# Chunked attention and a two-layer MLP on one core: 15 instead of 10 blocks of the first layer in seven products whose sums stay in PSUM, and a new order of all steps

## The chip, the cores and the metric

The kernel runs on one core of a Trainium2 chip (trn2). The metric is the device time of one execution in microseconds (us); lower is better.

## The reference

Heads of 64 columns, chunks of 64 tokens; the attention's output is the input of a two-layer MLP with a leaky ReLU between.

```python
q, k, v: (8, 8, 576, 64) float32              # batch, heads, tokens, columns
scores = q_c @ k_c.T / 8, per chunk of 64     # 9 chunks per batch and head
attn = exp(scores - max); attn /= sum + 1e-9
x = (attn @ v_c), heads side by side          # (4608, 512)
h = x @ w_in                                  # (512, 2048)
out = maximum(0.01 * h, h) @ w_out            # (4608, 512) float32
```

## The kernel before

The 4608 tokens are 36 groups of 128 (two chunks). For a group `u` the steps are: load q and k (`load_qk`, "g", DMAs issued by POOL that also convert to fp16), turn them (on TensorE, "tq"/"tk", or by a transposing DMA on SP's queue, "tdq"/"tdk"), copy q into a zero-padded tile QZ ("q"/"cq"), scores ("s", tile Sp), maximum ("m"), subtraction ("b"), exponential ("x"), sum and reciprocal ("z"), scaling ("n", tile en), transposing the weights ("e"+"c", or by DMA "d"), product with v ("v", tile xp) and the copy into `xT` ("a").

The MLP goes over blocks of tokens: `BLOCKS = 2 * [128] + 17 * [256]`. The first layer is either plain (`mm1`, "M" and "A": out tile hT, then the leaky ReLU on ACT into gT, "G") or, for blocks 9 to 18, done as seven half-size products instead of eight (`wide`, "V", L416; j, half s of the hidden columns, product number n). Their operands are sums of quarters of the weights (`w_in_sum`, "WS") and of the tokens (`x_sums`, "xs"). There the products 1, 6, 7 and 4 accumulate in one PSUM bank (xbank). After 1, 6 and 7, ACT copies the bank to SBUF (`wide_x`, "lx", L447, tile xkeep); DVE adds products 2, 5 and 3 to those copies (`wide_m`, "la", L453); the leaky ReLU (`leaky`, "lp", L435) then reads the sums from SBUF. That is 20 passes over 128x512 values for a block.

The second layer of all 256-token blocks is in seven products in the same way (`product`, "R", L227; weight sums TW, "W"; token sums SG, "sum", L203; `combine`, "comb"); blocks 0 and 1 use plain products (`mm2`, "B", tile oP, L462).

`idle` ("i") issues products of a constant tile `warm` that nobody reads; its argument counts columns in units of 128, three to a product (L686).

Every engine and every queue works its instructions in program order; the program order is written out by hand in the string `ORDER`, read from left to right. `BANKS` says which of the PSUM banks a tile takes. POOL's DMAs share eight semaphores in turn, so that the ninth issue waits for the first one's landing. All POOL loads up to g8 are issued ahead of anything in `ORDER` (`LOADS`).

Of the kernel before, what the change touches and what calls it, by code (L numbers as in the profile page):

```python
# [16 lines left out]
def kernel(  # L17
# [9 lines left out]
    nc = tc.nc  # L27
# [14 lines left out]
    VL = (4, 5, 6, 7)  # L42
    UX = 9
    G = 2 * CH

    BLOCKS = 2 * [128] + 17 * [256]
    EARLY = (2, 3, 4)
    LAST = len(BLOCKS) - 1
    HF, HM = NFC // 2, d_model // 2
    W0 = 9  # L50
    AMID = range(W0, 17)
    ONE = EARLY + tuple(range(16, len(BLOCKS)))
    ZMM = range(W0 - 2, 16)

# [3 lines left out]


# [5 lines left out]
    xT = sbp.tile([128, NT, RING], FP16, name="xT")  # L65
    qk: dict[int, tuple[bass.AP, bass.AP]] = {}

    made: set[tuple] = set()

    def need(*what):  # L70
        assert what in made, what

    def load_qk(u):

        both = []
        for name, src in (("q_in", q), ("k_in", k)):
            if u in PAIRED:
                t = sbp.tile([CH, H, 2, D], FP16, name=name, tag=name + "2", bufs=len(PAIRED))
            else:
                t = sbp.tile([128, H, D], FP16, name=name, tag=name, bufs=NIN)  # L80
            r0, r1 = u * G, (u + 1) * G
            cut = min(-(-r0 // S) * S, r1) if r0 % S else r1
            for a, z in ((r0, cut), (cut, r1)):
                if a < z:
                    rows = src[a // S, :, a % S:a % S + z - a, :]
                    if u in PAIRED:
                        to = t[(a - r0) // 2:(z - r0) // 2].rearrange("p h r d -> p h (r d)")
                        rows = rows.rearrange("h (p r) d -> p h (r d)", r=2)
                    else:
                        to, rows = t[a - r0:z - r0], rows.rearrange("h p d -> p h d")  # L90
                    nc.gpsimd.dma_start(out=to, in_=rows)  # L91
            both.append(t)
        qk[u] = tuple(both)

    def load_v_heads(b, m, h0, h1):
        if b >= NVB:
            need("batch", b - NVB)
# [4 lines left out]

    def load_v(b):
# [3 lines left out]
    def load_w_in(f0, f1):  # L107
        for m in range(2):
            nc.gpsimd.dma_start(
                out=w_inT[m * CH:(m + 1) * CH, :, f0:f1],  # L110
                in_=moe_w_in[m * d_model // 2:(m + 1) * d_model // 2, f0:f1].rearrange("(t d) f -> d t f", d=D),
            )

    def load_w_in_quarter(a):
        load_w_in(512 * a, 512 * a + 512)

    def load_w_out_quarter(a):
        load_w_out(4 * a, 4 * a + 4)
# [45 lines left out]
    SG: dict[tuple[int, int], bass.AP] = {}
    bank: dict[tuple[int, str], bass.AP] = {}
    kept: dict[tuple[int, str], bass.AP] = {}
    opened: set[tuple[int, str]] = set()

    def weight_sum(n):
        b11, b12 = w_outT[:, :HF, :HM], w_outT[:, :HF, HM:]  # L170
        b21, b22 = w_outT[:, HF:, :HM], w_outT[:, HF:, HM:]
        x, y = {1: (b12, b11), 2: (b22, TW.get(1)), 3: (b22, b12), 4: (b21, TW.get(2))}[n]
        TW[n] = sbp.tile([128, HF, HM], FP16, name=f"TW{n}")
        nc.vector.tensor_tensor(out=TW[n], in0=x, in1=y, op=ALU.subtract)

    def rows(j):

        nh = BLOCKS[j] // 2
        halves_of = slice(0, nh), slice(nh, 2 * nh)
        return halves_of[::-1] if j in EARLY else halves_of  # L180

    def token_sums(j, n):
        if (j, n) in SG:
            return
        if j in EARLY:
            for a, p in {
                1: [(a, 1) for a in range(4)], 2: [(0, 2), (1, 2)], 3: [(0, 1), (1, 1), (0, 2), (1, 2)], 4: [(2, 2), (3, 2)],
            }[n]:
                need("act", j, a, p)
        if n in (2, 4):  # L190
            token_sums(j, n // 2)
        nh = BLOCKS[j] // 2
        one, two = rows(j)
        a11, a12 = gT[j][:, :HF, one], gT[j][:, HF:, one]
        a21, a22 = gT[j][:, :HF, two], gT[j][:, HF:, two]
        SG[j, n] = sbp.tile([128, HF, nh], FP16, name="SG", tag="gS", bufs=4, padded_shape=[128, HF, 128])
        x, y, op = {
            1: (a21, a22, ALU.add),
            2: (SG.get((j, 1)), a11, ALU.subtract),
            3: (a11, a21, ALU.subtract),  # L200
            4: (a12, SG.get((j, 2)), ALU.subtract),
        }[n]
        (nc.gpsimd if (j, n) in SG_POOL else nc.vector).tensor_tensor(out=SG[j, n], in0=x, in1=y, op=op)  # L203

    def product(j, n, i):
        one, two = rows(j)
        g, w = gT[j], w_outT
        where, left, right = {
            1: ("X", g[:, :HF, one], w[:, :HF, :HM]),
            2: ("W", g[:, HF:, one], w[:, HF:, :HM]),  # L210
            3: ("Z", SG.get((j, 4)), w[:, HF:, HM:]),
            4: ("X", g[:, HF:, two], TW.get(4)),
            5: ("Z", SG.get((j, 1)), TW.get(1)),
            6: ("X", SG.get((j, 2)), TW.get(2)),
            7: ("X", SG.get((j, 3)), TW.get(3)),
        }[n]
        if where != "X" and j in ONE:
            where = n
        if (j, where) not in bank:
            tag = None if j in EARLY else {"X": "qp", "Z": None if j in ZMM else "kp"}.get(where)  # L220
            bank[j, where] = psp.tile([128, 2, HM], FP32, name=f"pr{where}", tag=tag or mm(), bufs=1)
        to = bank[j, where]
        if j == LAST and n == 4:
            last_product(left, right)
            return
        for f in range(HF):
            nc.tensor.matmul(  # L227
                out=to[:, i, :],
                lhsT=left[:, f, i * 128:(i + 1) * 128],
                rhs=right[:, f, :],  # L230
                start=(j, where) not in opened,
                stop=(f == HF - 1),
                skip_group_check=True,
            )
            opened.add((j, where))

    def last_product(left, right):

        r0 = START[LAST] + BLOCKS[LAST] // 2
        for c in range(0, HM, HM // 2):  # L240
            cut = slice(c, c + HM // 2)
            of = psp.tile([128, HM // 2], FP32, name="prL", tag=mm(), bufs=1, padded_shape=[128, 512])
            for f in range(HF):
                nc.tensor.matmul(
                    out=of, lhsT=left[:, f, :128], rhs=right[:, f, cut], start=(f == 0), stop=(f == HF - 1)
                )
            to = ob[LAST, False][:, 0, cut]
            nc.vector.tensor_tensor(out=to, in0=of, in1=kept[LAST, 7][:, 0, cut], op=ALU.add)
            nc.sync.dma_start(out=out[r0:r0 + 128, cut], in_=to)

    def combine(j, n):
        made.add(("comb", j, n))
        if n == 3 and j in ONE:
            need("comb", j, 0)
        nt = BLOCKS[j] // 256
        half = lambda t: t[:, :nt, :]
        keep = lambda: sbp.tile([128, 1, HM], FP32, name="keep", tag="k_in2" if n == 6 else "q_in2", bufs=len(PAIRED))
        if n in (1, 6, 7):
            kept[j, n] = keep()
            nc.scalar.activation(out=half(kept[j, n]), in_=half(bank[j, "X"]), func=AFT.Copy, bias=0.0, scale=1.0)  # L260
            return
        if n == 0:

# [609 lines left out]
```

## Time and profile before

| what | value |
|---|---|
| time, median of 3 runs | 275.1 us (274.96 to 275.74) |
| span of the profiled execution, first to last instruction | 273.3 us |
| the median less that span (the page gives no other time of the profiled execution) | 1.8 us |
| TensorE busy | 265.9 us, 97%, 3705 products |
| DVE, ACT, POOL busy | 219.9 us (80%), 208.8 us (76%), 165.3 us (60%) |
| POOL's DMA queue | 18.10 MB |
| granted TensorE clock | full in each of the 40 slices |

A row of the page's groups reads: line, engine, operation, output<-input, shape, count, busy time in all, mean of one in ns, idle time of the engine ahead of them and who ended it. PE is TensorE's products, PEld its weight loads. A product's time in such rows includes its latency, so the pace of products is read from the chain of waits, where products follow each other.

### The profile page before, as it was taken

To read this page: it belongs to the slowest core of one execution; us is meant where nothing else is said; L and a number is where in the kernel's file an instruction comes from. 1 tells how busy PE (TensorE), PEld (TensorE's weight loads), DVE (VectorE), ACT (ScalarE), POOL (GpSimd) and SP (SyncE) were. 2 spreads that over 40 slices of the span, in tenths; PEclk is the share of its full clock that TensorE was granted. 3 is DMA by queue.
4 is the path that set the end of the run, shared out by engine and by line. 5 is a ranking of instruction groups with operands and counts; after the bars stand their busy time and mean duration, and the time that the engine had idled before them with its cause. 6 is when DMAs were issued, how large, how long until landed. Compare 5 with 4: busy or idle time off the path is not lost.

```text
span 273.3 us, 9009 instructions
## 1 busy us (share of the span) xinstructions
PE 265.9 (97%) x3705; PEld 242.4 (89%) x3705; DVE 219.9 (80%) x427; ACT 208.8 (76%) x410; POOL 165.3 (60%) x190
## 2 busy tenths in 40 slices
PE   7889999999999999999999999999999999999994
PEld 3579958999999899998989999999999998999994
DVE  7786869999997668798677987977899879488783
ACT  6667635665779688666999989899999998857560
POOL 8848546783175448649689799689895636012100
PEclk9999999999999999999999999999999999999999
DMA  9999999999999999999999999799999503131113
GB/s 147 155 188 191 206 178 156 176 117 130 210 138 169 171 140 119 195 219 168 164 189 153 203 160 124 139 134 180 95 147 158 134 2 101 22 98 40 41 41 115
DMA packets 159241, 38.34 MB, mean 140 GB/s; under 512 B 150240, under 2 KB 154720, under 8 KB 159200
## 3 DMA queue, kind: packets, MB, share of 16 engines
q0 software_dynamic: 111392, 18.10, 98.3%
q1 hardware_dynamic: 46768, 19.41, 38.7%
q8 instruction: 29, 0.48, 0.7%
q10 hardware_dynamic: 1040, 0.26, 0.4%
q14 instruction: 12, 0.10, 0.2%
HBM read 36.70 MB, written 9.44 MB: 169 GB/s over the span
## 4 chain that ended last, share of the span: by engine, by line
PE 86%; DVE 5%; ACT 3%; POOL 3%; issue 2%; POOLq 0%; DVEq 0%; ACTq 0%
PE hT L319 20%; PE prX L227 20%; PE xbank L416 11%; PE xpr L416 9%; PE prZ L227 6%; PE pr L227 6%; PE prW L227 3%; PE Sp L584 3%; PE xp L656 3%; PE oP L462 3%; ACT QZ L539 1%; ACT gT L435 1%; PE kp L512 1%; PE qp L512 1%; POOL SG L203 1%
## 5 line engine op out<-in xcount | busy, mean ns | idle before, releaser
L319 PE MATMUL hT<-xT,w_inT 128*128 128x128 f16 (+1 forms) x768 | 62.4, 237 | 0.0
L319 PEld LDWEIGHTS <-w_inT 128*128 128x128 f16 x768 | 53.6, 98 | 2.8
L227 PEld LDWEIGHTS <-SG 128*128 128x128 f16 x544 | 51.0, 98 | 5.4
L620 POOL TENSOR_TENSOR en<-ex,zi 128x512 f16<-128x512 f16 x26 | 28.2, 1085 | 40.1 <-DVE zi L614 19.8
L453 DVE TENSOR_TENSOR xkeep<-xpr,xkeep 128x512 f32<-128x512 f32 x60 | 39.6, 681 | 13.7 <-ACT xkeep L447 9.6
L333 ACT ACTIVATE gT<-hT 128x512 f16<-128x512 f32 x64 | 36.6, 595 | 9.0 <-PE hT L319 8.9
L227 PEld LDWEIGHTS <-gT 128*128 128x128 f16 x400 | 37.3, 98 | 4.3 <-ACT gT L435 0.4
L447 ACT ACTIVATE xkeep<-xbank 128x512 f32<-128x512 f32 x60 | 34.6, 593 | 7.4 <-PE xbank L416 7.0
L416 PEld LDWEIGHTS <-WS 128*128 128x128 f16 x640 | 38.0, 98 | 0.5
L91 POOL DMA_DIRECT2D q_in<-in_q_dram x39 | 33.4, 861 | 7.0 <-DMA w_outT<-in_moe_w_out_dram 3.0
L91 POOL DMA_DIRECT2D k_in<-in_k_dram x39 | 32.6, 838 | 7.8 <-DMA VB<-in_v_dram 3.3
L227 PE MATMUL prX<-TW,SG 128*128 128x256 f16 x272 | 35.3, 273 | 0.0
L435 ACT ACTIVATE gT<-xkeep 128x512 f16<-128x512 f32 x56 | 33.4, 631 | 2.1 <-DVE xkeep L453 1.8
L260 ACT ACTIVATE keep<-prX 128x256 f32<-128x256 f32 x51 | 19.6, 384 | 16.9 <-PE prX L227 16.5
L416 PEld LDWEIGHTS <-w_inT 128*128 128x128 f16 x480 | 29.0, 98 | 0.9 <-issue 0.4
L203 DVE TENSOR_TENSOR SG<-gT 128x1024 f16<-128x1024 f16 x34 | 25.2, 740 | 4.7 <-ACT gT L333 2.9
L610 DVE TENSOR_REDUCE z<-ex 128x8 f32<-128x512 f16 x36 | 24.4, 679 | 4.9 <-ACT ex L604 4.7
L593 DVE TENSOR_REDUCE mx<-Sp 128x8 f32<-128x512 f32 x36 | 24.4, 677 | 4.5 <-PE Sp L584 4.5
L573 ACT ACTIVATE QZ<-QT 64x512 f16<-64x512 f16 x44 | 27.3, 627 | 0.9 <-PE Sp L584 0.3
L677 ACT ACTIVATE xT<-xp 128x512 f16<-128x512 f32 x36 | 21.5, 596 | 6.0 <-PE xp L656 5.8
L387 POOL TENSOR_TENSOR xs<-xT 128x256 f16<-128x256 f16 x18 | 12.5, 701 | 20.7 <-ACT xT L677 20.7
L98 POOL DMA_DIRECT2D VB<-in_v_dram x24 | 23.4, 987 | 0.0
(92 smaller groups left out, 486.0 us busy)
## 6 DMA issues: line engine op xcount, KB each, us to landing
out_dram<-osb SPq DMA_DIRECT2D x35, 256.0 KB, 4.1
q_in<-in_q_dram POOLq DMA_DIRECT2D x31, 128.0 KB, 5.9
k_in<-in_k_dram POOLq DMA_DIRECT2D x31, 128.0 KB, 6.7
VB<-in_v_dram POOLq DMA_DIRECT2D x8, 288.0 KB, 9.1
VB<-in_v_dram POOLq DMA_DIRECT2D x16, 144.0 KB, 5.3
w_inT<-in_moe_w_in_dram POOLq DMA_DIRECT2D x8, 256.0 KB, 7.2
w_outT<-in_moe_w_out_dram POOLq DMA_DIRECT2D x4, 512.0 KB, 11.6
q_in<-in_q_dram POOLq DMA_DIRECT2D x8, 64.0 KB, 6.3
```

The source lines that it names most:

```text
L91: nc.gpsimd.dma_start(out=to, in_=rows)
L203: (nc.gpsimd if (j, n) in SG_POOL else nc.vector).tensor_tensor(out=SG[j, n], in0=x, in1=y, op=op)
L227: nc.tensor.matmul(out=to[:, i, :], lhsT=left[:, f, i * 128:(i + 1) * 128], rhs=right[:, f, :], start=(j, where) not in opened, stop=(f == ...
L319: nc.tensor.matmul(out=hT[:, i, :], lhsT=w_inT[:, t, fc * 128:(fc + 1) * 128], rhs=xT[:, t, r0:r0 + tb], start=(t == 0), stop=(t == NT - 1),)
L333: nc.scalar.activation(out=gT[j][:, nf * a:nf * a + nf, c0:c0 + tb], in_=HT.pop((j, a, p)), func=AFT.Prelu, bias=0.0, scale=1.0, alpha=0.01,)
L416: nc.tensor.matmul(out=to[:, i, :], lhsT=left[:, t, i * 128:(i + 1) * 128], rhs=right[:, t], start=(n in (1, 2, 5) and t == 0 and i == 0), ...
L435: nc.scalar.activation(out=gT[j][:, f0:f0 + 4, hi * 128:hi * 128 + 128], in_=of, func=AFT.Prelu, bias=0.0, scale=1.0, alpha=0.01)
L447: nc.scalar.activation(out=XK[j, s, n], in_=XB[j, s], func=AFT.Copy, bias=0.0, scale=1.0)
L453: nc.vector.tensor_tensor(out=to, in0=of, in1=to, op=ALU.add)
L573: nc.scalar.activation(out=to, in_=QT[u][part], func=AFT.Copy, bias=0.0, scale=1.0)
L593: nc.vector.tensor_reduce(out=MX[u], in_=SP[u], axis=AXL.X, op=ALU.max)
L620: (nc.gpsimd if u >= UP else nc.vector).tensor_tensor(out=E[u], in0=ex, in1=ZI.pop(u).unsqueeze(2).to_broadcast((128, 8, CH)), op=ALU.mult)
```

## The change

First layer: blocks 3 to 17 (15 blocks) in seven products; blocks 0 to 2 plain, in pieces of 128 tokens. All blocks have 256 tokens, so the second layer of all 18 is in seven products. In the first layer product 2 now accumulates onto a copy of product 1 in another PSUM bank ("ls", `wide_seed`); product 5 is copied to SBUF once ("lf", `wide_five`); DVE makes two sums per half ("la", `wide_add`), one of them back into the PSUM bank on which product 3 then accumulates. The leaky ReLU reads PSUM or the one copy. That is 16 passes for a block. A step marked with ' in `ORDER` goes to the other engine of its kind (ACT or DVE for copies, POOL or DVE for sums and "n"). Any of the eight PSUM banks may hold any tile (`ps`), and `sb` picks an SBUF slot by a digit of `BANKS`, too.

```diff
-    BLOCKS = 2 * [128] + 17 * [256]
-    EARLY = (2, 3, 4)
+    BLOCKS = 18 * [256]
+    LATE = (0, 1, 2)
+    def ps(shape, name, kind=FP32):
+        ...
+        return psp.tile(shape, kind, name=name, tag="m" + next(banks), bufs=1, padded_shape=padded)
+    def copy(other, to, of):
+        if other:
+            nc.vector.tensor_copy(out=to, in_=of)
+        else:
+            nc.scalar.activation(out=to, in_=of, func=AFT.Copy, bias=0.0, scale=1.0)
-    def wide_x(j, s, n):
-        ...
-        nc.scalar.activation(out=XK[j, s, n], in_=XB[j, s], func=AFT.Copy, bias=0.0, scale=1.0)
-    def wide_m(j, s, n):
-        ...
-        nc.vector.tensor_tensor(out=to, in0=of, in1=to, op=ALU.add)
+    def wide_seed(j, s, other=0):
+        XW[j, s] = ps([128, 4, 128], "seed")
+        copy(other, XW[j, s], XB[j, s])
+    def wide_five(j, s, other=0):
+        X5[j, s] = sb([128, 4, 128], FP32, "x5", "xkeep", 6)
+        copy(other, X5[j, s], XZ[j, s])
+    def wide_add(j, s, n):
+        to = XZ[j, s] if n == 3 else X5[j, s]
+        nc.vector.tensor_tensor(out=to, in0=XB[j, s], in1=X5[j, s], op=ALU.add)
+    def wide_leaky(j, s, n, other=0):
+        second, hi = {2: (0, 0), 4: (0, 1), 3: (1, 0), 5: (1, 1)}[n]
+        of = {2: XW, 4: XB, 3: XZ, 5: X5}[n][j, s]
+        ...
     ORDER = (
-        "i33 y4 y2 I y0 y6 y1 tq0 q0.0 q0.1 w3 tk0 i5 k0 i6 s0 tq1 i4 m0 b0 q1.1.1 i13 tk1 q1.0.1 x0 k1 tq2 i8 s1 tk2 "
+        "g2 y4 y5' y0' i110.0 g1 I If g3 tq0 y2' tk0 y3' k0 tq2 q0.0 tk2 tq1 q0.1' s0 i16.4 k2 y1 i14.3 q2.0 q2.1' s2 "
+        "q1.0 m0 b0 q1.1 tk1 x0 k1 tq3 q3.1 g6 i8.2 tq6 tk3 tk6 g5 m2 b2 q3.0 z0.0 s1 tq5 i17.7 m1 tk5 b1 k3 z0.1' i25.5 "
```

Three places of the order show the move. First TensorE at the start of the program: before, the end of the first run of idle products, after 11 of them (warm is the constant tile, q_f and k_f the first group of q and k).

```order
L686 LDWEIGHTS warm
L686 MATMUL idle<-warm 128x384
L512 MATMUL qp<-ident_139,q_f 128x128 x4
L512 MATMUL kp<-ident_139,k_f 128x128 x4
L686 LDWEIGHTS warm
```

Now the same place, after 36 idle products of 384 columns and one of 256:

```order
L194 MATMUL idle<-warm 128x256
L222 MATMUL qp<-ident_85,q_f 128x128 x4
L222 MATMUL kp<-ident_85,k_f 128x128 x4
L227 LDWEIGHTS q_in
L227 MATMUL qp<-ident,q_in 64x2x32
```

The first transposition has moved behind 26 more idle products. Second, POOL's queue behind the third group of loads; before, v and all of w_in go ahead of w_out with nothing between:

```order
L98 DMA VB_63<-in_v_dram 64x36x64 x2
L109 DMA w_inT<-in_moe_w_in_dram 64x4x512 x4
L91 DMA q_in<-in_q_dram 64x8x64 x2
L91 DMA k_in<-in_k_dram 64x8x64 x2
L109 DMA w_inT<-in_moe_w_in_dram 64x4x512 x4
```

Now (en is the scaling of group 1, a POOL instruction that waits for DVE):

```order
L122 DMA VB_63<-in_v_dram 64x36x64 x2
L117 DMA q_in<-in_q_dram 64x8x64 x2
L117 DMA k_in<-in_k_dram 64x8x64 x2
L140 DMA w_inT<-in_moe_w_in_dram 64x4x512 x2
L309 TENSOR_TENSOR en<-ex,z_405 128x512
L140 DMA w_inT<-in_moe_w_in_dram 64x4x512 x2
L117 DMA q_in<-in_q_dram 128x8x64
L117 DMA k_in<-in_k_dram 128x8x64
L140 DMA w_inT<-in_moe_w_in_dram 64x4x512 x2
```

Two quarters of w_in and the loads behind them have moved behind a step that waits. Third, DVE in the middle of the program, before, with the adds of products 2, 5 and 3:

```order
L281 TENSOR_TENSOR osb_3871<-prW,keep 128x256
L453 TENSOR_TENSOR xkeep<-xpr,xkeep 128x512
L610 TENSOR_REDUCE z<-ex 128x8
L612 TENSOR_TENSOR ze<-z,tiny 128x8
L614 RECIPROCAL zi<-ze 128x8
L203 TENSOR_TENSOR SG<-gT 128x1024
L598 TENSOR_TENSOR Sp<-Sp,mx 128x512
```

Now, where DVE also copies:

```order
L461 TENSOR_TENSOR x_3657<-xbank,x_3657 128x512
L198 COPY seed<-xbank 128x512
L461 TENSOR_TENSOR xz<-xbank,x_3796 128x512
L299 TENSOR_REDUCE z_3830<-ex 128x8
L198 COPY keep<-prX 128x256
L305 RECIPROCAL z_3838<-z_3835 128x8
L461 TENSOR_TENSOR xz<-xbank,x_3840 128x512
L418 TENSOR_TENSOR xs<-xT 128x256
```

Copies from PSUM and token sums have come to DVE; the small add ahead of the reciprocal has gone to ACT.

More of the change, by code (lines that the diff above doesn't have):

```diff
@@ L176, in rows @@
[L176 to L183, printed above, removed]
-            return
[L185 to L235, printed above, removed]
@@ L497, with idle @@
+    def idle(n, _=0):
+        t = ps([128, 512], "idle")
+        for i in range(0, n, 3):
+            c = 128 * min(3, n - i)
+            nc.tensor.matmul(out=t[:, :c], lhsT=warm[:, :128], rhs=warm[:, :c], start=True, stop=True)
+    def copy(other, to, of):
+        if other:
+            nc.vector.tensor_copy(out=to, in_=of)
+        else:
+            nc.scalar.activation(out=to, in_=of, func=AFT.Copy, bias=0.0, scale=1.0)
     QP: dict[int, bass.AP] = {}
@@ L735, with stage_a, hidden, part_of @@
-    ORDER = (
[84 rows of a table removed]
+    def stage_a(u, other=0):
+        at = u * G % RING
+        copy(other, xT[:, :, at:at + G], XP[u])
+        groups.add(u)
+    gT: dict[int, bass.AP] = {}
+    HT: dict[tuple[int, int, int], bass.AP] = {}
+    def hidden(j):
+        if j not in gT:
+            gT[j] = sb([128, NFC, BLOCKS[j]], FP16, "gT", "gT", 3, padded_shape=[128, NFC, NB])
+        return gT[j]
+    def part_of(j, p):
+        return (128, (p - 1) * 128) if p else (BLOCKS[j], 0)
+    def mm1(j, a, p=0):
+        tb, c0 = part_of(j, p)
+        rows_ready(START[j] + c0, START[j] + c0 + tb)
+        r0 = (START[j] + c0) % RING
+        nf = 512 // tb
+        hT = ps([128, nf, tb], "hT")
+        for i in range(nf):
+            fc = nf * a + i
+            for t in range(NT):
+                nc.tensor.matmul(
+                    out=hT[:, i, :],
+                    lhsT=w_inT[:, t, fc * 128:(fc + 1) * 128],
+                    rhs=xT[:, t, r0:r0 + tb],
+                    start=(i == 0 and t == 0),
+                    stop=(t == NT - 1),
+                    skip_group_check=True,
+                )
+        HT[j, a, p] = hT
@@ new lines, in halves_of, with token_sums @@
+    def halves_of(j):
+        both = slice(0, 128), slice(128, NB)
+        return both[::-1] if j in LATE else both
+    def token_sums(j, n, other=0):
+        one, two = halves_of(j)
+        g = hidden(j)
+        a11, a12 = g[:, :HF, one], g[:, HF:, one]
+        a21, a22 = g[:, :HF, two], g[:, HF:, two]
+        x, y, op = {
+            1: (a21, a22, ALU.add),
+            2: (SG.get((j, 1)), a11, ALU.subtract),
+            3: (a11, a21, ALU.subtract),
+            4: (a12, SG.get((j, 2)), ALU.subtract),
+        }[n]
+        SG[j, n] = sb([128, HF, 128], FP16, "SG", "gS", 5)
+        (nc.gpsimd if other else nc.vector).tensor_tensor(out=SG[j, n], in0=x, in1=y, op=op)
```

702 lines of the change are left out of this document (280 added, 422 removed), and 172 rows, old and new, of the table ORDER.

## The prediction

> **What bounds the kernel now.** I read the page's busy times first, then a table of five stretches, then the list of waits.
>
> ```profile
> PE 265.9 (97%) x3705; PEld 242.4 (89%) x3705; DVE 219.9 (80%) x427; ACT 208.8 (76%) x410; POOL 165.3 (60%) x190
> PEclk9999999999999999999999999999999999999999
> ```
>
> ```profile
> core 0: us, PE busy (x) PEld busy (x) DVE busy (x) ACT busy (x) POOL busy (x), PEclk, DMA share, GB/s
> 0.00:20.00 20.00, 16.41 (x237) 11.16 (x238) 15.66 (x33) 12.96 (x19) 14.26 (x25) 1.00 1.62 162
> 20.00:60.00 40.00, 40.00 (x603) 35.48 (x601) 32.80 (x62) 24.93 (x50) 28.17 (x34) 1.00 1.98 172
> 60.00:130.00 70.00, 70.00 (x852) 64.16 (x851) 57.51 (x115) 51.17 (x101) 40.15 (x44) 1.00 1.79 165
> 130.00:200.00 70.00, 69.82 (x1041) 66.15 (x1040) 57.12 (x111) 66.02 (x133) 59.14 (x65) 1.00 1.54 154
> 200.00:270.00 70.00, 69.66 (x985) 65.41 (x983) 56.74 (x107) 53.76 (x111) 23.56 (x25) 1.00 0.46 77
> ```
>
> From 20 to 270 us TensorE is idle for 0.52 us in all (0.18 + 0.34). So the end is set by two things only: how many products there are and at what pace they go, and what the first 20 us hold. The pace stands in the chain of waits, where products follow each other:
>
> ```profile
> 22.68 3.58 PE hT L319 x64
> 37.58 4.32 PE oP L462 x20
> 90.16 0.87 PE prX L227 x8
> 145.25 0.89 PE xbank L416 x16
> ```
>
> A product of 128 columns takes 55.9 ns (3.58/64, and 0.89/16 in the seven-product layer), one of 256 columns 109 ns (0.87/8), one of 512 columns 216 ns (4.32/20). Time goes by columns, with a little on top for each product.
>
> **The change: TensorE's work.** Counts are from code and order, prices from the rows above.
> - First layer. Before: 512 products of 128 columns (plain, in pieces), 256 of 256 (blocks 5 to 8), 1120 of 128 (ten blocks of 112). After: 384 plain of 128 and 15 x 112 = 1680. That is 432 more of 128 columns (+24.1 us) and 256 fewer of 256 columns (-27.9): -3.8 us.
> - Second layer. 1000 products of 256 columns instead of 944 (+6.1), none of the 32 of 512 columns (-6.9): -0.8 us.
> - Three groups less are turned on TensorE, 24 products of 128 columns: -1.3 us. Three groups more go by SP's transposing DMAs, and SP issues nothing else that early.
>
> The sum is -5.9 us. Scores, v products and the six groups whose weights TensorE turns stay.
>
> **The change: idle products.** The start reads:
>
> ```profile
> 1.33 3.50 PE L686 MATMUL idle<-warm 128*128 128x384 f16 x11 [1.33 <-DVE zeros L137]
> 4.71 0.63 PE L512 MATMUL qp<-ident,q_f 128*128 128x128 f32 x4
> 11.59 2.07 PE L686 MATMUL idle<-warm 128*128 128x384 f16 x13
> 17.44 1.95 PE L319 MATMUL hT<-xT,w_inT 128*128 128x128 f16 x32
> 20.05 1.06 PE L319 MATMUL hT<-xT,w_inT 128*128 128x128 f16 x16
> ```
>
> The first 11 idle products take 0.32 us each (3.50/11). The later 13, which hold 29 units of 128 columns, take 2.07, with the last one's latency: at most 71 ns a unit. I take 54 ns a unit (a quarter of the 216 above). The orders hold 111 units before and 239 after. Before: 3.5 + 78 x 0.054 = 7.7 us. After: the first run is 110 units, so 33 units go in 3.5 us and 77 in 4.2, to 9.0 us; the other 129 units take 7.0. In all 14.7 us, +7.0 us. This is the largest loss: the first transposition, which began at 4.71 us when its data had come, begins at 9.0.
>
> The Trainium skill (TensorE: Matmul & The Clock Gate, What's actually happening) says that the clock opens after about 3.4 us of work, in a window that runs free of the kernel. The trace agrees: slow to 4.8 us, fast behind. Should the window fall later, some ten more of the long first run would go at 0.32 instead of 0.16: +1.6 us. I do not count it; before, that would have hidden behind the wait for q.
>
> **The change: waits at the start.** Before, from 1.33 to 20.05 us: 18.7 us, of which 7.7 idle products and 6.1 of use (32 first-layer products 1.8, the rest turns, scores, v): 4.9 us are waits. The chain behind them:
>
> ```profile
> 7.87 0.69 DVE L593 TENSOR_REDUCE mx<-Sp 128x8 f32<-128x512 f32 x1 [0.50 <-PE Sp L584]
> 8.25 1.49 ACT L539 ACTIVATE QZ<-qp 64x512 f16<-64x512 f16 x2 [1.50 <-PE qp L517]
> 8.60 0.69 DVE L598 TENSOR_TENSOR sh<-Sp,mx 128x512 f32<-128x512 f32 x1
> 9.61 0.60 ACT L604 ACTIVATE ex<-sh 128x512 f16<-128x512 f32 x1
> 10.24 0.69 DVE L610 TENSOR_REDUCE z<-ex 128x8 f32<-128x512 f16 x1 [0.95 <-ACT ex L604]
> 13.28 0.67 DVE L620 TENSOR_TENSOR en<-ex,zi 128x512 f16<-128x512 f16 x1
> ```
>
> With these prices I put the new order's steps behind each other by hand, each when its engine and its input are free: scores of group 0 at 11.3 us (behind k's copy and q's cast on ACT, 0.6 each, from 10.0), of group 2 at 13.2, of group 1 at 15.4; scaling of group 0 done at 18.2, of group 1 (on POOL) at 20.4, of group 2 at 22.9; v products at 20.9, 23.6 and 24.4; copy of group 1's result, behind an exponential on ACT, done at 25.1. The first first-layer product goes at 25.2, where work and idle products alone come to 22.5, and one more wait of 0.35 follows. So 3.1 us of waits: -1.8 us. Much of what was waiting is idle products now.
>
> **What hides the rest.** ACT loses 60 copies of 593 ns and gains 47 like them; DVE keeps 60 adds.
>
> ```profile
> L453 DVE TENSOR_TENSOR xkeep<-xpr,xkeep 128x512 f32<-128x512 f32 x60 | 39.6, 681 | 13.7 <-ACT xkeep L447 9.6 <-PE xpr L416 3.9
> L447 ACT ACTIVATE xkeep<-xbank 128x512 f32<-128x512 f32 x60 | 34.6, 593 | 7.4 <-PE xbank L416 7.0 <-DMA out_dram<-osb 0.2
> L203 POOL TENSOR_TENSOR SG<-gT,SG 128x1024 f16<-128x1024 f16 x8 | 17.4, 2173 | 9.3 <-DVE SG L203 4.0 <-ACT keep L260 2.7 <-ACT xkeep L447 2.6
> L260 ACT ACTIVATE keep<-prX 128x256 f32<-128x256 f32 x51 | 19.6, 384 | 16.9 <-PE prX L227 16.5
> L387 DVE TENSOR_TENSOR xs<-xT 128x256 f16<-128x256 f16 x2 | 0.6, 282 | 0.0
> L387 POOL TENSOR_TENSOR xs<-xT 128x256 f16<-128x256 f16 x18 | 12.5, 701 | 20.7 <-ACT xT L677 20.7
> L541 DVE COPY QZ<-qp 64x512 f16<-64x512 f16 x19 | 7.9, 417 | 1.8 <-ACT QZ L539 1.5 <-PE qp L512 0.2
> L612 DVE TENSOR_TENSOR ze<-z,tiny 128x8 f32<-128x8 f32 x36 | 6.6, 182 | 1.2
> L281 DVE TENSOR_TENSOR osb<-prZ,keep 128x256 f32<-128x256 f32 x22 | 9.3, 421 | 4.6 <-PE prZ L227 3.1 <-ACT keep L260 1.2
> L620 POOL TENSOR_TENSOR en<-ex,zi 128x512 f16<-128x512 f16 x26 | 28.2, 1085 | 40.1 <-DVE zi L614 19.8 <-ACT xkeep L447 9.8 <-ACT gT L435 3.0
> ```
>
> DVE gains 19 copies of 256 values (0.42 each, 8), 19 of 512 (0.68, 13), 29 short token sums (0.28, 8); it gives away 8 long sums (0.7), 25 small adds (0.18), 15 q copies (0.42) and 4 clearings, some 19 in all. With some 2 us of small ones: about 232 us, 86% of 270. ACT comes to some 203, POOL to 184 (12 long sums more at 2.17). None passes TensorE; the same DVE held 82% from 20 to 60 and from 60 to 130 us while TensorE stood still for nothing. A copy from PSUM to PSUM is not in the trace: 0.38 us (half the columns, to SBUF) and 0.68 (the DVE add) bound it; I take the 0.593 of the same read. At 26 on ACT the ends are -5.5 and +2.3 us of ACT time, under 203 of 272: no cost to TensorE.
>
> In the order, between a product and the next that needs its bank read out, at least 1.3 us of other products stand now, 0.87 before. So I take 0.3 us of late waits instead of 0.52: -0.2. The last product, the two adds behind it and the two small stores stay as they were.
>
> **Sum.** -5.9 + 7.0 - 1.8 - 0.2 = -0.9: a span of 272.4 against 273.3. With the 1.8 us by which the median stands over that span: 274.2 us.
>
> **Rivals.**
>
> 1. The shared port makes it slower. One row pair shows what it costs:
>
> ```profile
> 204.40 1.98 DVE L203 TENSOR_TENSOR SG<-gT 128x1024 f16<-128x1024 f16 x1
> 204.76 1.06 POOL L620 TENSOR_TENSOR en<-ex,zi 128x512 f16<-128x512 f16 x1
> ```
>
> A DVE sum of two SBUF tiles, begun just ahead of a POOL instruction, ends only behind it: 1.98 us instead of about 0.7. POOL's sums and scalings grow to 20 long ones (2.17), 25 scalings (1.09) and 27 short (0.7): 89 us of 270, a third of the time, beside some 110 such DVE steps. Were they placed without regard to each other, about 36 would be hit. A hit lasts up to 2.2 us and the least distance on TensorE is 1.3, so up to 0.9 reaches TensorE each; if a sixth of them do that, +5.4 us: 279.6. Two that reach TensorE already end the gain. Against it: the order before has 70 such POOL steps, and TensorE idles for half a microsecond.
>
> The Trainium skill (SBUF — State Buffer, Who interferes with whom) states it as a rule: the port pair is an exclusive lock, and a DVE step with both inputs in SBUF blocks against a GpSimd step that reads SBUF. The trace agrees with the pair above. By that rule, more long sums on POOL speak against this change.
>
> 2. The start costs less: my hand chain has waits that cover each other, since q's first copies no longer stand behind the clearing of tiles on DVE. With 1.1 us of waits at the start instead of 3.1: 272.2.
>
> 3. The transfers are not further ahead where it counts: the second quarter of w_in now stands on POOL's queue behind the scaling of group 1.
>
> ```profile
> 15.02 0.68 POOL L91 DMA_DIRECT2D k_in<-in_k_dram  x1 [2.17 <-DMA VB<-in_v_dram]
> w_inT<-in_moe_w_in_dram POOLq DMA_DIRECT2D x8, 256.0 KB, 7.2
> ```
>
> In my chain POOL comes to that scaling at 15.3 us and may run it only at 19.4, so that quarter is issued until 21.7 and lands, with the 7.2 us of the row, at 28.9, where TensorE wants it at 28.8; each us on it is lost. Two us late: 276.2. For it: POOL waits for DMAs at the start as it is (2.17 us in one place). Against it: the queue has drained by then, so the landing should be quicker.
>
> **How the numbers follow.** The sum holds within a microsecond or so: 0.5. Shorter start: 0.18. Port: 0.2. Late weights: 0.12. Changes under 0.3% (0.8 us) can hardly be told from none, so the likeliest case lies on the edge: of its 0.5, 0.28 is faster, 0.18 the same, 0.04 slower. Faster: 0.28 + 0.17 = 0.45. Same: 0.18 + 0.01 + 0.04 = 0.23. Slower: 0.2 + 0.08 + 0.04 = 0.32. The likeliest case by itself spans 273.0 to 275.6. The range goes from 271.0 (all waits gone: -5.9 + 7.0 - 4.9 - 0.3 = -4.1) to 280.0 (the port's 279.6).
>
> **What would show it.** Right: TensorE's first transposition near 9 us and its first first-layer product near 25; from there on TensorE idle for under a microsecond; plain products near 56 ns. Wrong: idle of TensorE behind DVE sums or seeds in the middle (port, or the 128-column products at more than 56 ns), first-layer products waiting for w_in before 35 us, or a first transposition well before 9 us.

## The result and the profile after

The changed kernel takes 301.2 us (298.8 to 304.2), the kernel before 275.1 us beside it: a ratio of 1.091 (1.086 to 1.095), 9% slower where 274.2 us was forecast. The profiled execution is the longest of the four: 304.2 us, span 302.3. Here and below, a time is the median of all executions of a kernel and a ratio leaves out those more than 1.5% above its fastest, so the two can differ a little.

The first part of the page, busy times and granted clock:

```profile
PE 273.7 (91%) x3924; PEld 250.2 (83%) x3924; DVE 228.3 (76%) x456; ACT 203.0 (67%) x408; POOL 182.3 (60%) x192
PEclk9999999999999999999989999999997999999999
```

The table by stretches, cut as before (the last row is longer now):

```profile
core 0: us, PE busy (x) PEld busy (x) DVE busy (x) ACT busy (x) POOL busy (x), PEclk, DMA share, GB/s
0.00:20.00 20.00, 16.76 (x200) 10.77 (x201) 8.64 (x18) 12.36 (x20) 14.71 (x24) 1.00 1.91 156
20.00:60.00 40.00, 36.43 (x632) 33.63 (x628) 34.58 (x68) 32.13 (x66) 25.40 (x30) 1.00 1.49 150
60.00:130.00 70.00, 61.13 (x883) 56.54 (x884) 56.87 (x120) 50.94 (x103) 49.53 (x55) 1.00 2.03 147
130.00:200.00 70.00, 62.64 (x908) 58.37 (x907) 55.21 (x112) 51.94 (x106) 49.77 (x50) 0.98 1.76 165
200.00:270.00 70.00, 67.86 (x972) 64.33 (x970) 54.79 (x106) 44.37 (x92) 35.53 (x31) 0.98 0.55 86
```

DVE, ACT and POOL are as busy as forecast. TensorE is not: from 20 to 270 us it stands still for 3.57 + 8.87 + 7.36 + 2.14 = 21.9 us, where before it was 0.5. That is most of the 29.0 us by which the span grew. Three quarters of it (16.2 us) lie between 60 and 200 us, while loads are under way (POOL's last one lands at 228 us). The chain of waits, by engine:

```profile
PE 50%; DMA 27%; DVE 10%; ACT 9%; issue 3%; SPq 1%; DVEq 0%; ACTq 0%
```

TensorE had 86% of it before, and DMA none. Five of the chain's long pieces (start, length, what):

```profile
83.91 7.86 DMA et<-en
...
97.14 10.09 DMA KT<-k_in
...
109.63 10.27 DMA et<-en
...
130.62 9.36 DMA QT<-q_in
...
141.36 8.17 DMA et<-en
```

All three names are transposing DMAs that SP issues: et turns a group's weights, QT and KT turn q and k. The waits of TensorE (total, times, longest):

```profile
PE xp L335 <- DMA et<-en: 13.4, 8, 2.3
PE prX L525 <- DVE keep L198: 2.1, 1, 2.1
PE Sp L277 <- DMA KT<-k_in: 2.1, 2, 1.5
PE Sp L277 <- DVE ob L563: 1.4, 1, 1.4
```

More than half of the idle time is named by one transfer. From the parts on DMA issues, first of the kernel before, then of the changed one (count, KB each, median us from issue to landing):

```profile
q_in<-in_q_dram POOLq DMA_DIRECT2D x31, 128.0 KB, 5.9
et<-en SPq DMA_TRANSPOSE x30, 5.2
QT<-q_in SPq DMA_TRANSPOSE x22, 5.1
KT<-k_in SPq DMA_TRANSPOSE x22, 5.2
```

```profile
q_in<-in_q_dram POOLq DMA_DIRECT2D x31, 128.0 KB, 10.4
et<-en SPq DMA_TRANSPOSE x30, 7.9
QT<-q_in SPq DMA_TRANSPOSE x25, 7.7
KT<-k_in SPq DMA_TRANSPOSE x25, 8.4
```

The same transposing DMAs take half as long again, the loads of q three quarters longer. I followed et's way through both traces between 60 and 180 us, medians: from the end of the scaling to SP's issue 0.8 us before, 2.5 after; in flight 5.4 and 8.2; from issue to the use on TensorE 9.7 and 9.6. So et had 3.3 us to spare and has 0.8, and 12 of 30 have less than one. By these medians the products come as far behind the issue as they did, and the transfers became longer; the 9.6 holds some of TensorE's own waits, since in 8 of the 30 groups the use came right at the landing. SP's queue issues later because it stands longer for loads. Its waits for q, in the kernel before and in the changed one:

```profile
SPq L564 <- DMA q_in<-in_q_dram: 9.3, 5, 3.2
```

```profile
SPq L264 <- DMA q_in<-in_q_dram: 26.1, 8, 12.1
```

Loads wait for transposing DMAs in turn: POOL loads q into a buffer again only when the old q has been turned.

```profile
POOL q_in L117 <- DMA QT<-q_in: 21.9, 7, 6.5
```

### The profile page after: what moved, and what is told of

Same layout as the page of the kernel before. It is cut to its first block, busy times and chain, and to the rows that moved or that the text cites. A ratio compares the mean times of both kernels' runs of the same rounds, so it can differ in the third digit from the quotient of the medians.

```text
span 302.3 us, 9517 instructions
## 1 busy us (share of the span) xinstructions
PE 273.7 (91%) x3924; PEld 250.2 (83%) x3924; DVE 228.3 (76%) x456; ACT 203.0 (67%) x408; POOL 182.3 (60%) x192
## 4 chain that ended last, share of the span: by engine, by line
PE 50%; DMA 27%; DVE 10%; ACT 9%; issue 3%; SPq 1%; DVEq 0%; ACTq 0%
DMA et<-en 15%; PE prX L525 13%; PE xbank L442 11%; PE prZ L525 7%; DMA KT<-k_in 6%; PE xz L442 4%; PE prW L525 4%; DMA QT<-q_in 3%; PE idle L194 3%; PE seed L442 3%; DMA out_dram<-ob 3%; ACT gT L384 3%; ACT QZ L200 2%; DVE SG L502 2%; PE xp L335 2%
## 5 line engine op out<-in xcount | busy, mean ns | idle before, releaser
L442 PEld LDWEIGHTS <-WS 128*128 128x128 f16 x960 | 59.9, 100 | 2.7 <-issue 0.9
L525 PEld LDWEIGHTS <-SG 128*128 128x128 f16 x576 | 54.2, 98 | 8.3 <-issue 2.3
L117 POOL DMA_DIRECT2D q_in<-in_q_dram x39 | 33.5, 862 | 29.2 <-DMA QT<-q_in 21.9
L442 PEld LDWEIGHTS <-w_inT 128*128 128x128 f16 x720 | 45.6, 99 | 1.4 <-issue 0.4
L525 PEld LDWEIGHTS <-gT 128*128 128x128 f16 x424 | 39.7, 98 | 3.9
L525 PE MATMUL prX<-TW,SG 128*128 128x256 f16 x288 | 37.6, 275 | 2.3 <-DVE keep L198 2.1
L442 PE MATMUL xbank<-xs,WS 128*128 128x128 f16 x480 | 37.3, 224 | 0.3 <-ACT seed L200 0.3
L309 POOL TENSOR_TENSOR en<-ex,z 128x512 f16<-128x512 f16 x25 | 26.3, 1061 | 12.9 <-DVE z L305 6.9
L502 POOL TENSOR_TENSOR SG<-gT 128x1024 f16<-128x1024 f16 x7 | 15.4, 2199 | 27.2 <-DVE ob L563 11.7
L335 PE MATMUL xp<-et,VB 128*128 128x64 f16 x288 | 14.0, 193 | 14.4 <-DMA et<-en 13.4
L200 ACT ACTIVATE xT<-xp 128x512 f16<-128x512 f32 x30 | 17.6, 595 | 12.6 <-PE xp L335 12.5
L384 ACT ACTIVATE gT<-xbank 128x512 f16<-128x512 f32 x30 | 17.8, 596 | 12.1 <-PE xbank L442 11.9
L563 DVE TENSOR_TENSOR ob<-prZ,keep 128x256 f32<-128x256 f32 x36 | 14.9, 419 | 14.0 <-PE prZ L525 6.3
L461 DVE TENSOR_TENSOR x<-xbank,x 128x512 f32<-128x512 f32 x30 | 20.5, 684 | 6.5 <-PE xbank L442 6.5
L335 PEld LDWEIGHTS <-VB 128*128 128x128 f16 x288 | 11.7, 98 | 16.4 <-DMA et<-en 11.0
```

Of the source, the lines that this page charges most:

```text
L200: nc.scalar.activation(out=to, in_=of, func=AFT.Copy, bias=0.0, scale=1.0)
L309: (nc.gpsimd if other else nc.vector).tensor_tensor(out=EN[u], in0=EX[u], in1=Z[u, 2].unsqueeze(2).to_broadcast((128, 8, CH)), op=ALU.mult)
L335: nc.tensor.matmul(out=XP[u][:, t, e, :], lhsT=VB[b % NVB][:, t, c, :], rhs=ET[u][:, t // 2, e, t % 2, :], start=(e == 0 and t == 0), stop ...
L384: nc.scalar.activation(out=to, in_=of, func=AFT.Prelu, bias=0.0, scale=1.0, alpha=0.01)
L442: nc.tensor.matmul(out=to[:, i, :], lhsT=left[:, t, i * 128:(i + 1) * 128], rhs=right[:, t], start=(n in (1, 5) and t == 0 and i == 0), st ...
L461: nc.vector.tensor_tensor(out=to, in0=XB[j, s], in1=X5[j, s], op=ALU.add)
```

## The experiments

Unless it says otherwise, each kernel is the changed one with the edit shown. "Under way" is the mean number of POOL's loads in flight between 60 and 140 us, "flight" the median of the transposing DMAs issued then, both worked out from the issue and landing times in the traces:

| kernel | us | ratio | under way | flight us | TensorE behind et, us |
|---|---|---|---|---|---|
| before | 275.1 | 1 | 2.9 | 5.3 | 0 |
| changed | 301.2 | 1.091 | 6.7 | 8.6 | 13.4 |
| most of v not loaded | 286.4 | 1.032 | 3.0 | 6.3 | 4.8 |
| and k loaded once | 287.5 | 1.044 | 1.2 | 3.7 | 3.7 |
| 13 groups turned on TensorE | 293.5 | 1.069 | 3.9 | 6.3 | none |
| loads paced | 301.0 | 1.093 | 3.8 | 6.6 | 5.7 |
| loads first | 295.7 | 1.068 | 5.9 | 8.4 | 7.6 |
| POOL loads only, early | 294.6 | 1.065 | 4.9 | 8.2 | 6.4 |
| that, v not loaded | 283.4 | 1.029 | 3.0 | 6.3 | 2.1 |
| softmax ahead, loads first | 310.2 | 1.122 | 3.4 | 5.9 | 0.3 |
| before, loads held back | 279.7 | 1.017 | 3.3 | 5.8 | 0.5 |

**Fewer loads.** The loads of v behind the first two batches are dropped (20 of 24), so this kernel leaves out a part of the result.

```diff
- L2 L3 vl4.0 vl4.1 vl5.0 vl5.1 vl6.0 vl6.1 vl7.0 vl7.1
```

> The changed kernel without the loads of V for batches 2 to 7 (20 of its 24 V transfers; the later batches are multiplied with the V of the first two, so this part of the result is left out). Nothing else moves on any engine. Theory A (the transposing DMAs et, QT and KT share the DMA engines with 6 to 7 loads under way, land in a median 8 us instead of the 5.2 of before, and TensorE stands in front of them for most of its 32 us of gaps): a fifth fewer load packets, transposing DMAs land in about 6.5 us, the gaps fall to about 18 us, time 285 to 291 us. Theory B (the order places each transposing DMA too near its use, and SP issues them one by one; traffic matters little): 297 to 301 us, landing unchanged at about 8 us.

286.4 us (283.1 to 290.2), ratio 1.032 (1.028 to 1.036). What is left of TensorE's waits for et:

```profile
PE xp L335 <- DMA et<-en: 4.8, 3, 2.0
```

Taking the loads of v away, with the order of everything else kept, gives back 15 of 26 us. Over the whole run et is back at its old flight (5.3 us, 5.2 before); between 60 and 140 us the transposing DMAs still take 6.3 instead of 5.3. The edit takes two things away at once: the transfers, and POOL's time to issue them (rows of v's loads: 23.6 us before the edit, 5.0 after). Then k is also loaded only once into each of its eight buffers, which leaves out more of the result:

```diff
+            elif name == "k_in" and slot in k_loaded:
+                both.append(k_loaded[slot])
```

> As the run without the later V loads, and besides K is loaded only once into each of its 8 buffers (the later groups are multiplied with old K and old V, so this part of the result is left out); all transposing DMAs, stores and engine instructions stay. Theory A: some 40% fewer load packets, at most 3 loads under way as in the kernel before, transposing DMAs land in 4 to 5 us, the gaps fall below 10 us, time 272 to 280 us, which is then the sum of the prediction without the late transfers. Theory B: still over 294 us.

287.5 us, ratio 1.044 (1.042 to 1.046): no better, and far from the 272 to 280 expected, though et lands in 3.5 us, quicker than before the change. The waits:

```profile
PE xp L344 <- DMA et<-en: 3.7, 2, 2.0
PE prW L534 <- DVE ob L572: 2.5, 1, 2.5
PE xbank L451 <- DVE x L470: 2.5, 2, 2.2
```

So flight is not all. Some 12 us over the kernel before stay when the transfers are fast; the waits seen are for two et that SP issues late and for DVE steps. One DVE sum of this run took 4.54 us where its like takes 0.68: it began at 103.28 us, while POOL was issuing a load, and ended 0.57 us behind the two POOL sums that followed.

**et taken off the queue.** 13 of the early groups are turned by TensorE and copied by ACT, as six were (for all of groups 6 to 9, 11 to 13, 15 to 17 and 19 to 21). Two of the turned tiles lie in PSUM banks whose next use is a seed, so the sums of groups 12 and 18 start from other numbers; the work is the same.

```diff
- d6 ... d21
+ e6 c6 ... e21 c21
```

> Thirteen of the early groups (6 to 9, 11 to 13, 15 to 17, 19 to 21) have their en turned on TensorE with a copy by ScalarE, as groups 0 to 5 have, instead of by a transposing DMA; placed about 2 us of TensorE work ahead of the value products. Costs 13 x 4 x 56 ns = 2.9 us of TensorE. Theory A and B alike (it is the flight of et that TensorE waits for, 13.4 us by the list of waits): 288 to 292 us. Theory C (loads as a whole come too late, and TensorE only meets that lack at the value products; the wait goes on to Sp and QZ, that is to KT, QT and q_in): 297 to 302 us.

293.5 us, ratio 1.069 (1.064 to 1.074). No wait for et is left, and the clock stays full, but the waits are now these:

```profile
PE prX L525 <- DVE keep L198: 2.1, 1, 2.1
PE xp L335 <- ACT gT L384: 2.1, 1, 2.1
PE xbank L442 <- DVE x L461: 1.9, 1, 1.9
```

With all 13.4 us of them gone the kernel is 7.7 us faster, after paying some 3 us for TensorE's own turns; other waits have come in for the rest. Here the loads stay, and POOL's steps with them, so this gain comes by way of et alone.

**Why the loads are late or many.** Scaling 1 on POOL, ahead of half of w_in and of the loads behind it, waits 5.95 us for DVE at the start. It goes to DVE:

```diff
- n1'
+ n1
```

> The multiply of group 1 (the first on POOL) goes to VectorE, so that POOL's loads of w_in and of groups 7 to 9 are not queued behind its wait of 5.95 us for VectorE at 15.8 to 21.8 us. Theory D (the load queue loses 6 us there, and all later loads, which are bound by the DMA engines, come that much later): 293 to 296 us. Theory A without D (the backlog later, not its start, sets the landing times): 298 to 301 us; the loads only stand in the queue earlier.

298.0 us, ratio 1.078 (1.071 to 1.085): et waits 6.8, 6.1 loads under way. Helps a little. Next, POOL reads the k of two groups earlier before it issues a pair of loads, so that fewer are under way:

```diff
+        if len(asked) >= 12:
+            nc.gpsimd.tensor_copy(out=pace, in_=qk[asked[-2]][1][:, 0, :8])
+        asked.append(u)
```

> The changed kernel, in which POOL reads 8 columns of the k_in loaded two groups earlier before it issues the next group's loads of q and k (from the thirteenth load on), so that about 4 loads of q and k are under way at a time instead of 6 to 7; the order is otherwise the same. Theory A with too many loads under way as its cause (the DMA engines are shared out among what is under way, and loads that are issued earlier only lengthen the flight of the transposing DMAs): transposing DMAs land in 5 to 6.5 us, 285 to 293 us. Theory E (the DMA engines are at their limit between 60 and 200 us, so what is held back is simply late): transposing DMAs land no sooner than in 7 us or q_in lands later, and the time is 299 us or more.

301.0 us, ratio 1.093 (1.087 to 1.099). The flights shorten to 6.1 for et, TensorE waits 5.7 us for it instead of 13.4, and the time is the same: POOL, held up, is late elsewhere.

```profile
PE xp L341 <- DMA et<-en: 5.7, 6, 1.8
PE prX L531 <- POOL SG L508: 3.3, 1, 3.3
PE Sp L283 <- DMA KT<-k_in: 2.8, 2, 1.5
```

Then w_out's four loads right behind the tenth group's, with scaling 1 on DVE:

```diff
- n1' ... g10 n5' ... P0 ... P1 ... P3 ... P2
+ n1 ... g10 P0 P1 P2 P3 n5'
```

> The multiply of group 1 goes to VectorE as in the run before, and the four loads of w_out are issued right after those of group 10, ahead of POOL's multiplies of groups 5 and 4, for which they stood waiting until 39 to 43 us. Theory D (POOL's queue, in which loads stand behind multiplies that wait, starts the backlog): w_out lands 6 to 8 us earlier, the three late value products between 50 and 60 us (4 us of gaps) go, all later loads come some 6 us earlier, 289 to 294 us. Theory A alone: 296 to 300 us, since the late transfers between 80 and 180 us stay.

295.7 us, ratio 1.068 (1.060 to 1.076). That with the 13 turns (copies on ACT and DVE by turns):

> As the run with w_out's loads first, and the thirteen early groups turned on TensorE (copies by ScalarE and VectorE in turn). If the late et and the queue of loads are two causes that add up: 282 to 287 us (the former run's time, less some 10 us of waits for et, plus 2.9 us of TensorE). If both only move the same backlog: 288 to 293 us. In neither case below the 275 us of the kernel before.

294.9 us, ratio 1.070 (1.066 to 1.075): the two edits don't add up. With scalings 5 and 6 on DVE as well, POOL does nothing but load early:

```diff
- n5' ... n6'
+ n5 ... n6
```

> The changed kernel in which POOL does nothing but loads until 60 us: the multiplies of groups 1, 5 and 6 go to VectorE, and w_out's loads follow those of group 10. Theory D (POOL's loads fall behind in the first 60 us, 11 loads of K against 14 in the kernel before, and this lag is what keeps 6 to 7 loads under way until 140 us and makes the transposing DMAs long): by 80 us nearly as many loads have landed as before (19), et lands in 5 to 6.5 us, the waits for et fall below 3 us, 285 to 290 us. Against it (the lag is made good, but the order asks for groups 9 to 20 while loads and transposing DMAs are both under way, which the kernel before does not): 293 to 297 us, as with w_out's loads first.

294.6 us, ratio 1.065 (1.058 to 1.072). By 80 and 100 us 19 and 22 loads of q have landed, as many as before the change, yet 4.9 loads are under way and the flight is 8.2 us. That, without the loads of v behind the first two batches:

> As the run in which POOL does nothing but loads until 60 us, and without the loads of V for batches 2 to 7 (that part of the result is left out). If late transfers are the whole of the loss, early and later ones, both remedies add up, and what is left is the prediction's sum (274.2 us) with the 2 to 3 slowed operations of VectorE (4 us): 276 to 280 us. If something else in the order holds TensorE up: 283 to 287 us, no better than without V alone.

283.4 us, ratio 1.029 (1.024 to 1.034), the least of the changed versions, with part of the loads missing. That is the outcome put down for the case that something else in the order holds TensorE up: both remedies together do not bring the 276 to 280 us of late transfers alone. Its waits:

```profile
PE xbank L442 <- DVE x L461: 3.1, 1, 3.1
PE xp L335 <- DMA et<-en: 2.1, 2, 1.1
```

The other side of it: the kernel before, with POOL held up at groups 8 to 12 so that its loads fall behind as in the changed one.

```diff
+        if 8 <= u <= 12:
+            nc.gpsimd.tensor_copy(out=pace, in_=qk[asked[-2]][1][:, 0, :8])
```

> The kernel before, with its order and its first layer, in which POOL reads 8 columns of the k_in loaded two groups earlier before it loads groups 8 to 12, so that its loads fall behind by some 6 us (about 3 groups) between 35 and 60 us, as those of the changed kernel do. Theory D: transposing DMAs of the kernel before land in 7 to 8 us instead of 5.2 between 60 and 140 us, eat up its 3.3 us of margin, and it gets 5 to 15 us slower: 280 to 290 us. Against it (the order before has slack in every place): 275 to 278 us.

279.7 us, ratio 1.017 (1.011 to 1.023). By 60 us 12 loads of q have landed instead of 16, and the transposing DMAs go in 5.8 us, not 8. A late start of the loads therefore does not by itself make the flights long; that theory falls. The last of this kind, the version with POOL loading only, with the loads from group 13 on up to 4 us later:

> The run in which POOL does nothing but loads until 60 us (294.6 us), in which from group 13 on the loads of q and k then stand up to 4 us later in POOL's queue, without a wait added. Theory A (at equal throughput, loads that are issued earlier only stand longer under way and lengthen the transposing DMAs beside them): loads under way between 60 and 140 us fall from 4.9 towards 3.5, transposing DMAs from 8.2 to about 6.5 us, 287 to 291 us. Against it (the loads are only just in time now, and what is issued 4 us later lands later): 295 to 300 us.

301.8 us, ratio 1.094 (1.091 to 1.097): 3.7 loads under way, flight 7.0, but 10.2 us of waits for et in three places, and only 16 loads of q landed by 80 us. Fewer under way by holding back costs more than it brings: 294.6 us without it.

**Idle products.** The first run is cut to 60 units, the others are left out.

```diff
- i110.0 i16.4 i14.3 i8.2 i17.7 i25.5 i23.6 i8.1 i13.9 i5.8
+ i60.0
```

> The changed kernel with 60 units of idle products at the start instead of 110, and none of the 129 units after that; 179 x 56 ns = 10 us of TensorE work left out. The prediction's term (idle products more than before cost 7.0 us): 291 to 295 us. Rival (they only stand in waits that are there anyway, for the first loads, for QZ and for the exponents): 299 to 302 us, with gaps in their place; above 302 if the granted clock falls behind them.

297.9 us (292.7 to 299.6), ratio 1.068 (1.058 to 1.077). Of some 10 us of products left out (179 units at 55 ns or so) 3 are gained by the medians and some 6 by the ratios (1.091 and 1.068); waits take the place of the others, and the clock is at half for longer, 23.9 us of the profiled execution against 6.8. Two stretches of this run:

```profile
13.00:23.30 10.30, 6.40 (x75) 5.49 (x74) 8.82 (x19) 8.85 (x18) 7.60 (x12) 0.50 1.75 157
57.40:60.80 3.40, 3.40 (x30) 2.87 (x27) 2.50 (x6) 1.18 (x2) 1.71 (x2) 0.50 2.63 153
```

**The same order with more room for et.** The sums of the exponents with their reciprocals, the scalings and et's transposing DMAs of groups 9 to 35 are moved 8 us ahead; the same on the version with the loads first; and there 12 us.

```diff
- z9.1' z9.2 ... n9' ... d9
+ (each as far ahead as its input and buffers allow, at most 8 us)
```

> The changed kernel in which, for groups 9 to 35, the small steps behind the exponent (sum, 1e-9, reciprocal, the multiply to en) and the transposing DMA of en stand 8 us earlier in the order, as far as the exponent is done by then; the buffers of z, en and et are handed out anew for it, the rest of the order is untouched and no instruction is added. Theory F (the order leaves 8 to 10 us from the multiply to the value products, and a transposing DMA beside the loads takes all of that; the room was there, since in the trace the exponents of groups 14 and 16 to 27 are done 5 to 28 us ahead of the multiply): the waits for et between 100 and 180 us go (8 us), 290 to 295 us. Theory E (loads and DMA engines set when the groups come, so an earlier multiply changes little): 298 to 302 us.

> The same 8 us on top of the kernel whose w_out loads stand ahead of POOL's first multiplies (295.7 us). Theory F: the 7.6 us of waits for et go, 285 to 290 us; what is left then are waits for VectorE behind its slowed operations (2 places of 2 us). Theory E: 294 to 297 us.

> As the run before with 12 us instead of 8. Theory F: no more than 2 us below the run with 8 us, since a transposing DMA lands within 10 us; if VectorE or POOL are asked for the small steps too early, they wait for the exponents and hold up the sums behind them: then 2 us or more above it.

309.4, 310.2 and 319.3 us, ratios 1.119, 1.122 and 1.155 (each within 0.007). In the second TensorE waits for et only once, 0.3 us, and has these waits instead:

```profile
PE prX L525 <- POOL SG L502: 6.6, 4, 2.4
PE Sp L277 <- DVE ob L563: 3.8, 1, 3.8
```

Then only SP's queue, its steps sorted by when their input is ready, on the changed kernel and on the one with POOL loading only.

```diff
- W1.1 d6 ... R1.5 d8 tdq12
+ n6' d6 ... n8 d8 tdq12
```

> The changed kernel with SP's queue alone in another order up to 200 us: its transposing DMAs and stores stand in the order in which their inputs were there in the trace of the changed kernel (the transposing DMA of en is counted 1 us earlier), so that none stands behind one that waits for its load. In the changed kernel 2.5 us pass from the end of the multiply to the issue of et (median between 60 and 180 us; 0.8 in the kernel before). Theory G (SP's queue is half of what makes et late): that falls to about 1 us, the waits for et from 13.4 to about 6 us, time 292 to 296 us. Against it (only the flight counts, and what is brought forward on SP pushes another transposing DMA back): 299 to 303 us.

> Both: POOL does nothing but loads until 60 us (294.6 us alone), and SP's queue stands in the order in which the inputs were there in that run. Theory G: 287 to 291 us. Against it: 294 to 297 us.

310.0 and 305.0 us, ratios 1.116 (1.109 to 1.124) and 1.107 (1.099 to 1.116). In the first et's waits fall to 3.1 us; ACT, which wants QT, now waits, and TensorE for ACT. It also has 23.9 us at half the clock, 17.1 more than the changed kernel; at half speed that is 8.5 us, as much as lies between the two (8.8 by the medians, 7.0 by the profiled spans). The other five re-orderings have 10.2 to 20.5 us at half.

```profile
ACT QZ L200 <- DMA QT<-q_in: 19.6, 6, 5.6
```

```profile
PE xbank L442 <- ACT seed L200: 4.6, 1, 4.6
PE prX L525 <- ACT gT L384: 4.5, 1, 4.5
```

## Why the prediction was wrong

**TensorE's work: right.** The useful products come to 6.8 us less, counted at the median distance of starts of each shape (255.8 and 249.0 us; 5.9 less forecast). The seven-product layer goes at the old pace: the chain after has `PE xbank L442 x16` in 0.89 us and `PE prX L525 x8` in 0.87.

**Idle products: the difference right, its parts not.** From each start to the next they take 9.7 us before and 16.6 after, some 7 more (7.0 forecast), but both sums are some 2 us above my working (7.7 and 14.7); waits behind them are in these sums, without them it is 8.4 and 16.2. The timeline of TensorE after, in its first 30 us:

```profile
1.32 9.02 PE L194 MATMUL idle<-warm 128*128 128x384 f16 x37 [1.32 <-DVE zeros L163]
10.18 0.60 PE L222 MATMUL qp<-ident,q_f 128*128 128x128 f32 x4
...
27.78 1.95 PE L370 MATMUL hT<-xT,w_inT 128*128 128x128 f16 x32 [0.34 <-ACT xT L200]
```

The first run took 9.02 us, not 7.7: the products quicken at 7.2 us instead of 4.5, a longer slow phase that the prediction had priced at +1.6 and not counted. The first transposition came at 10.2 instead of 9.0, the first first-layer product at 27.8 instead of 25.2.

**Waits at the start: not smaller.** The 4.9 us that I took for the kernel before were not there: by the table shown, TensorE was idle for 20 - 16.41 = 3.6 us up to 20 us, 1.3 of them ahead of its first product, so 2.3 behind it. After, it is idle for 2.5 us from its first product to the first first-layer product. The gain of 1.8 had nothing to come from. That product came 2.6 us later than forecast, about half of it by the longer first run.

**What hides the rest: totals right, the conclusion wrong.** DVE 228, ACT 203 and POOL 182 us were forecast at 232, 203 and 184; the copy from PSUM to PSUM takes 587 ns on ACT (593 taken). But the term "0.3 us of late waits instead of 0.52" measured 21.9, 13.4 of them behind et, and that is the step that failed. I took it from the distance between products on TensorE alone. An input that comes by a transposing DMA was never costed: neither its flight beside other transfers nor its place in SP's queue. "SP issues nothing else that early" was the only sentence on it. No rival named it either.

What the runs show in its place: 2.8 us more of flight take et's margin from 3.3 to 0.8 us, and 1.7 us more in SP's queue take up what distance the new order has (from the scaling to the use 11.5 us in the median, 10.2 before, some of it TensorE's own stalls). That the loads make the flight long is shown: take loads away, and it falls from 8.6 to 6.3 and 3.7 with the order unchanged. That late transposing DMAs cost time is shown twice: without most of v's loads the time falls by 15 us, and with 13 et off the queue, all loads kept, by 7.7 net. How much of the 15 belongs to POOL's time, which went with the loads, no run separates; and the second fall of the flight, to 3.7, gave no time at all. The clock (below) accounts for 3.4 us. That the rest is lost in DVE, ACT and POOL steps that come late because TensorE and the transfers are late is argued from the lists of waits, and not shown by a run.

**Rivals.** The weights (276.2) did not come late: no wait for w_in stands in the list. The shorter start did not occur. The port (279.6) did, in a small number of places, and more of DVE's time goes to it than before: its steps with more than 0.2 us over the median of their shape lose 8.5 us (9 steps), 5.0 before (7 steps). The worst place, DVE first, then POOL:

```profile
223.23 4.14 DVE L502 TENSOR_TENSOR SG<-gT 128x1024 f16<-128x1024 f16 x1
```

```profile
222.93 1.74 POOL L122 DMA_DIRECT2D VB<-in_v_dram  x2
224.67 2.15 POOL L502 TENSOR_TENSOR SG<-gT,SG 128x1024 f16<-128x1024 f16 x1
```

DVE's sum of 0.7 us begins during POOL's issue of two loads, lies beside its long sum, and ends 0.55 us behind that. TensorE waits 2.14 us for the copy that follows. The pair that the prediction shows from the kernel before is of this kind too; POOL was issuing a load when DVE's sum began at 204.40:

```profile
203.87 0.88 POOL L98 DMA_DIRECT2D VB<-in_v_dram  x1
```

In all three kernels looked at (before, changed, and the one without most of k and v) DVE's longest sum of two SBUF tiles is one that began during an issue of POOL. No run moved these steps apart, so what the port cost TensorE is read from waits alone.

**Open.** With loads as far ahead as before the change (POOL loading only) 4.9 are still under way against 2.9, and I did not find which move holds them there. The runs without loads keep 8 to 12 us over the kernel before. In their profiled executions (spans 9.8, 12.6 and 9.8 us over before's) TensorE is idle for 7.6, 10.1 and 7.0 us after the first 20, and the half clock takes 1.7, 1.7 and 3.4: nearly all of it. Slowed DVE steps and late et are among these waits; what starts each of them is open. No version that computes everything beat 294 us in its median, so none beats the kernel before.

## What to carry to other kernels

Cost every DMA whose result an in-order engine waits for: the queue that issues it, its flight beside all that is under way at that place, and the margin left, since the same distance in the order is not the same margin. When a kernel's engines all run in fixed orders with a microsecond or three to spare, one late transfer is not mended by moving steps: all six re-orderings of this kind (ratios 1.094 to 1.155) were slower than the version they started from, five of them with more time at half the clock as well. What helped was less for the DMAs to do (1.029 to 1.044 without loads, 1.069 with 13 turns on TensorE) and POOL's loads put ahead of its steps that wait (1.065 to 1.078).

## What was not expected of the hardware

**Flight of a transposing DMA.** One that is issued late in the program, with no load of POOL under way, lands in 2.3 to 2.5 us; with 1.2, 2.9 and 6.7 loads under way the medians are 3.7, 5.3 and 8.6. The numbers in between do not lie on a line (4.9 gives 8.2, but 4.4 in another run 6.9). The Trainium skill (DMA: Bandwidth & Descriptors, Queues, rings and completion order) says that each DMA engine serves the queues that have work in turn, a packet at a time. The trace agrees in so far as SP's transfers slow down beside POOL's loads.

**Short idle, half the clock.** TensorE's product behind the et of 141.36 us (in the chain above) began at 149.58 after 2.34 us of idle. The stretches around it:

```profile
144.00:147.00 3.00, 3.00 (x47) 2.82 (x46) 2.97 (x11) 2.98 (x7) 1.76 (x2) 1.00 2.14 136
147.00:149.40 2.40, 0.24 (x7) 0.11 (x4) 1.90 (x6) 1.07 (x3) 0.98 (x2) 1.00 1.50 124
149.40:150.60 1.20, 1.02 (x19) 0.99 (x20) 0.00 (x0) 0.58 (x2) 0.00 (x0) 0.99 2.42 154
150.60:154.00 3.40, 3.40 (x29) 3.09 (x27) 1.29 (x2) 1.98 (x5) 0.00 (x0) 0.50 1.92 195
```

The clock falls to half 1 us behind the idle time and stays there for 3.4 us, which costs 1.7 us more than the wait itself. The same follows the 2.14 us of idle at 225.6 (0.51 from 229.0 to 232.5). In the run with POOL loading only an idle of 2.9 us cost no clock.

Where the idle falls makes the difference. The four changes of the clock in the changed kernel (150.59, 154.00, 229.09, 232.50 us) lie whole steps of 3.41 us behind the start of full speed at 7.22. Cut into such steps, the whole 2.34 us lie in the step ahead of the first fall, and 2.1 us in the one ahead of the second; no other step of this trace, from 20 us to the last product, has more than 1.9. In the run with POOL loading only the step's edge cuts the 2.9 us in two (with other idle beside it, 1.63 and 1.49 us in the two steps), and the clock stays. Over the traces of all runs, each step at full clock with 1.95 us of idle or more was followed by half clock as long as products followed, and behind the first 20 us none with less than 1.9.

The Trainium skill (TensorE: Matmul & The Clock Gate, What's actually happening) puts the fall behind an idle window of about 3.4 us. The trace agrees on the 3.4 us and on a window that runs by itself, but an idle of some 2 us within one window was enough here.
